# Token products divided around a unit test, with filler products, one-hot rows in one operation, and signs, a table load and casts in other places

## The chip, the cores and the metric

The kernel runs on one core of one Trainium2 chip. The metric is device time of one execution in microseconds. TensorE (PE in the rows; PEld its weight loads), VectorE (DVE), ScalarE (ACT) and GpSimd (POOL) each work through their own queue in program order; SyncE (SP) issues most transfers.

## The reference, cut to what matters

Sparse attention (32-wide blocks, window 16) over 4 x 8 x 768 x 64 gives x of 3072 tokens by 512; a soft mixture of 32 slots in 8 experts follows; then a routed mixture:

```python
xn = x / (norm(x) + 1e-6);  en = emb / (norm(emb) + 1e-6)
logits = xn @ en.T / tau
expert_idx = argmax(logits, axis=1)
gate_w = softmax(logits)[arange(N), expert_idx]
for e in range(E):
    mask = expert_idx == e
    h = maximum(x[mask] @ w1[e], 0.0)
    out[mask] = gate_w[mask, None] * (h @ w2[e])
```

## The kernel before

The first part (to about 186 us) is attention and the soft mixture; the change leaves it alone. It leaves for every token 32 combination weights, transposed and split into parts, in `cT` (128 rows by 3072 tokens), so that x is `cT` times slot outputs, and the hidden layer of the routed part is `cT` times a matrix G with 1024 columns, one per hidden unit. The rest serves one expert for all tokens (an extra loop at the end, L1445 on, runs only for experts beyond the first; here it does not run).

Most units have one sign for all tokens and are folded into a linear part. The unit test finds the others in two levels, by matrix products and one-hot rows. **Level one** (L1126 to L1191): bounds per unit give `flag1`; the rank products `rank1` (L1161, L1163) count flagged units; `places1` (L1168) turns ranks into one-hot rows `OH1`, four 128-wide operations for each of two halves f (L1175), each multiplied by the unit's sign `ngs`; `candidates` (L1181) gathers the flagged columns of G into `Gc`, and `candidates_t` (L1187) the same transposed into `GNc`, with the unit's index and sign beside it. **Level two**: `tile_mm` (L1089) forms the hidden values of 128 candidates for 1024 tokens, six tiles in three double banks; `tile_ev` (L1099) reduces each tile, odd ones as a maximum on VectorE (L1103), even ones as Relu with a sum on ScalarE (L1105). `rank2`, `places2` and `mixed_units` (L1212, L1223, L1232) pick at most 96 mixed units, fetch their rows of w2 by an indirect DMA into `wr` (GpSimd, L1239), and put their columns into `Gm`. `lin` (L1205) is the linear part; its sum over rows, `prs` (L1338), is copied to the last 32 rows of `wr` (L1339).

**Beside the test** runs the routing. `tok` (L1193) has one product per 128 tokens, 24 of 40 columns, for norms and logits; `pl_out` (L1203) copies 12 at a time. `norms(0)`, `norms(1)` (GpSimd) multiply and add up a tree of halvings; `norms(2)` takes the square root (L966), `norms(3)` the reciprocal. `codes(0)` to `codes(6)` make the expert code and the gate: `codes(5)` is an Exp on ScalarE (L985), which needs another function table than the square root, `codes(6)` sums and inverts.

**Output** (L1356): for each of 24 tiles of 128 tokens three products of 512 columns (L1359 to L1361: `hi` by `wmh`, `lo` by `wmh`, `hi` by `wml`), a scaling by the gate, and a store of 256 KB. `mixed(i)` (L1326) makes `hi` and `lo` for 512 tokens. `wmh` and `wml` are `wr` rounded and its rest.

Order: the program has a manual schedule, so each engine runs in the order of the text. Products that serve no result stand in three places: `fill` (L1087), `warm2`, `warm3` (L1349). Filler products read `cT` and write a bank that nobody reads. Banks of PSUM pass from pool to pool tile by tile, so that a product into a reused bank waits for its last reader.

Of the kernel before, what the change touches and what calls it, by code (L numbers as in the profile page):

```python
# [11 lines left out]
F32 = mybir.dt.float32  # L12
# [10 lines left out]
P = 128  # L23
# [18 lines left out]
NPL = 96  # L42
# [94 lines left out]
def tile_kernel(ctx, tc, qT, kTd, vwd, phi, w1, w2, emb, tau, u1, u2, consts, consts2, out):  # L137
# [802 lines left out]
    cbx = fp.tile([P, 1], F32, name="cbx")  # L940
    base = fp.tile([P, 1], F32, name="base")
# [5 lines left out]
    def norms(i):  # L947

        if i < 2:
            for b in range(2 * i, 2 * i + 2):  # L950
                v = lambda a: a.rearrange("p (g j) s -> p g j s", j=2)
                nc.gpsimd.tensor_tensor(
                    out=v(sq[:, 6 * b : 6 * b + 6]),
                    in0=v(pl[:, 6 * b : 6 * b + 6, 0:NSLOT]),
                    in1=ce_all[:, b].rearrange("p (j g) s -> p g j s", g=3),
                    op=ALU.mult,
                )
        if i == 1:
            h = NSLOT // 2
            while h > 1:  # L960
                nc.gpsimd.tensor_add(sq[:, :, 0:h], sq[:, :, 0:h], sq[:, :, h : 2 * h])
                h //= 2
            nc.gpsimd.tensor_add(nrm, sq[:, :, 0], sq[:, :, 1])
        if i == 2:
            nc.vector.tensor_scalar_max(nrm, nrm, 0.0)
            nc.scalar.sqrt(nrm, nrm)  # L966
        if i == 3:
            nc.vector.tensor_scalar_add(nrm, nrm, 1e-6)
            nc.vector.reciprocal(nrm, nrm)
# [95 lines left out]
    junk = hhi[0].rearrange("p a b -> p (a b)")[:, 0:1024]  # L1065
# [6 lines left out]
    with ExitStack() as es:  # L1072
# [25 lines left out]

        def tile_ev(i, ph):  # L1099

            k, j = divmod(i, 3)
            if i % 2:
                nc.vector.tensor_reduce(acc[:, k, j : j + 1], ph, axis=AX.X, op=ALU.max)  # L1103
            else:
                nc.scalar.activation(junk, ph, AF.Relu, accum_out=acc[:, k, j : j + 1])  # L1105
# [20 lines left out]
        def flags(f):  # L1126
# [11 lines left out]
            b2 = lambda a: a.unsqueeze(2).to_broadcast([P, 4, 2])  # L1138
            nc.gpsimd.tensor_tensor(
                out=GN[:, ks, P : P + 2], in0=b2(con2[:, C_U + 4 * f : C_U + 4 * f + 4]), in1=b2(ngs[:, ks]),  # L1140
                op=ALU.mult,
            )

# [24 lines left out]
        def places1(f):  # L1168
            ks = slice(4 * f, 4 * f + 4)
            nc.vector.scalar_tensor_tensor(  # L1170
                out=rk[:, ks], in0=prk1[f][:, 0:4], scalar=1.0, in1=flag1[:, f, 0:4],
                op0=ALU.add, op1=ALU.mult,
            )
            for k in range(4 * f, 4 * f + 4):
                nc.vector.scalar_tensor_tensor(  # L1175
                    out=OH1[:, k], in0=iota, scalar=rk[:, k : k + 1], in1=ngs[:, k : k + 1].to_broadcast([P, P]),
                    op0=ALU.is_equal, op1=ALU.mult,
                )
            fits(cbs[:, f : f + 1], prk1[f][:, 4:5], P, cbs[:, 0:1] if f else cb)
# [7 lines left out]
        def candidates_t(f):  # L1187
            p = pgnc[:, f * (P + 2) : (f + 1) * (P + 2)]
            for k in range(4):
                nc.tensor.matmul(p, OH1[:, 4 * f + k], GN[:, 4 * f + k], start=k == 0, stop=k == 3)  # L1190
            return p  # L1191
# [31 lines left out]
        def places2(t):  # L1223
# [5 lines left out]
                out=OH2[:, t], in0=iota[:, 0:NPL], scalar1=rk2[:, ts], scalar2=None, op0=ALU.is_equal  # L1229
            )  # L1230

        def mixed_units(pf):  # L1232
            pix = pgm[0:NPL, 128:130]
            for t in range(2):
                nc.tensor.matmul(pix, OH2[:, t], GNc[:, t, P : P + 2], start=t == 0, stop=t == 1)
            nc.vector.tensor_scalar(
# [8 lines left out]
            fill(1, pf)  # L1245
# [29 lines left out]
        pls = [pre(4 + h, f"pls{h}")[:, 0 : 12 * NKL].rearrange("p (t x) -> p t x", x=NKL) for h in range(2)]  # L1275
        tok(0, 4)
        rank1(0)
        tok(4, 8)
        rank1(1)
        tok(8, 12)  # L1280
        pl_out(0)
        places1(0)
        tok(12, 18)
        candidates(0)
        places1(1)
        tok(18, 24)
        pl_out(1)
        candidates(1)
        es.close()
        ps2 = es.enter_context(tc.tile_pool(name="ps2", bufs=1, space=PSUM, reuse_waits="tile"))  # L1290
        norms(0)
        codes(0)
        linear_columns()
        norms(1)
        codes(1)
        for i in range(6):
            ph = tile_mm(i)
            tile_ev(i, ph)
            if i in (3, 5):
                if i == 3:  # L1300
                    pgnc = one(0, "pgnc")
                p = candidates_t(i // 4)
                nc.scalar.copy(GNc[:, i // 4], p)
            if i == 4:
                prk2 = dbank(0, "rank2")
                rank2(0)
        prr = one(1, "lin")
        lin(0)
        lin(1)
        rank2(1)  # L1310
        pf = dbank(1, "fill1")[:, 0:512]
        fill(1, pf)
        places2(0)
        places2(1)
        nc.scalar.copy(rs, prr)
        pgm = one(0, "pgm")
        mixed_units(pf)
        norms(2)
        fits(cbx, prk2[:, 2:3], NPL, cbs[:, 1:2])
# [25 lines left out]
    mixed(2)  # L1345
    codes(4)
    pw = bankc(6, "warm3")
    for _ in range(3):
        nc.tensor.matmul(pw, Gm, cTt(0, 512), start=True, stop=True)  # L1349
    nc.scalar.copy(wmh[:, c[0]], wr[:, c[0]])  # L1350
    nc.vector.tensor_copy(wmh[:, c[1]], wr[:, c[1]])
    for i in range(2):
        nc.vector.tensor_tensor(out=wml[:, c[i]], in0=wr[:, c[i]], in1=wmh[:, c[i]].bitcast(F32), op=ALU.subtract)
    codes(6)
    row_weights(cbx)
    for t in range(NTT):  # L1356
# [5 lines left out]
        if t % 4 == 1 and t // 4 + 3 < 6:  # L1362
            mixed(t // 4 + 3)
# [94 lines left out]
```

## Time and profile before

| | us |
|---|---|
| median of three runs | 245.72 (244.62 to 248.24) |
| profiled execution | 246.85 |
| its span, first to last instruction | 245.1 |
| TensorE busy, share of the span | 226.9 (93%) |
| VectorE, ScalarE, GpSimd busy | 150.7, 118.0, 94.2 |
| mean granted TensorE clock | 0.939 of full speed |

The profile is one execution. Its rows show busy times and waits of each engine; the granted clock is the share of TensorE's full speed that the chip gave in a stretch (1.00 or 0.50 here). A wait is put down to the instruction that released it last.

### The profile page before, as it was taken

How to read it: one execution, taken by the hardware profiler on the slowest of the kernel's cores; microseconds unless marked ns; L12 is line 12 of the kernel's file. 1: busy time of each engine (PE TensorE's matmuls, PEld its weight loads, DVE VectorE, ACT ScalarE, POOL GpSimd, SP SyncE). 2: the span in 40 equal slices, each digit the busy share in tenths (PEclk: the TensorE clock that was granted, in tenths of full speed). 3: DMA queues.
4: the chain of work that ended last, by engine and by line, in shares of the span. 5: the costliest groups of instructions: out<-in, count | busy, mean ns of one | idle time of the engine just before them, and what ended most of it. 6: DMA issues, size and time to landing. Idle time of an engine off the chain costs nothing.

```text
span 245.1 us, 7881 instructions
## 1 busy us (share of the span) xinstructions
PE 226.9 (93%) x3025; PEld 151.4 (62%) x3025; DVE 150.7 (61%) x709; ACT 118.0 (48%) x279; POOL 94.2 (38%) x147
## 2 busy tenths in 40 slices
PE   8798999999999999999999999999899999779970
PEld 3476877777768777677777543333254895257850
DVE  2348877769859798688875541128671646376740
ACT  2364466566656657565686311141322735346540
POOL 0264766557574775747663001000013374200000
PEclk9869999999999999999999999999999857758997
DMA  6999999999997999984499999999949400105992
GB/s 199 383 413 367 335 362 334 392 386 361 369 367 260 347 366 397 369 297 150 154 319 342 396 409 394 409 407 408 367 158 379 166 0 0 32 1 214 348 400 79
DMA packets 33658, 72.53 MB, mean 296 GB/s; under 512 B 2712, under 2 KB 4504, under 8 KB 33616
## 3 DMA queue, kind: packets, MB, share of 16 engines
q1 hardware_dynamic: 33552, 71.77, 79.8%
q8 instruction: 26, 0.43, 0.7%
q0 software_dynamic: 64, 0.20, 0.3%
q14 instruction: 16, 0.13, 0.1%
HBM read 65.67 MB, written 6.29 MB: 294 GB/s over the span
## 4 chain that ended last, share of the span: by engine, by line
PE 82%; DMA 7%; DVE 2%; SPq 2%; issue 2%; ACT 2%; POOL 1%; ACTq 0%; POOLq 0%; DVEq 0%
PE po L379 10%; PE s L324 9%; PE pt L366 8%; DMA vw<-in_vw_dram 7%; PE pO L856 6%; PE ph L777 6%; PE tx L412 5%; PE pv L272 4%; PE lp L430 4%; PE py L1359 3%; PE py L1360 2%; PE pd L284 2%; PE py L1361 2%; PE pa L487 2%; PE pls L1195 2%
## 5 line engine op out<-in xcount | busy, mean ns | idle before, releaser
L352 POOL TENSOR_TENSOR fix<-fix,nb 128x360 f32<-128x360 f32 x64 | 49.1, 788 | 49.1 <-DVE nb L339 48.9
L339 DVE CUSTOM_DVE_ANT_0 fix<-s,con 128x120 f32<-128x120 f32 x192 | 41.7, 278 | 18.0 <-PE s L324 14.4
L367 ACT COPY pts<-pt 120x384 f32<-120x384 f32 x64 | 27.7, 482 | 13.5 <-PE pt L366 13.5
L358 ACT ACTIVATE fix<-fix 128x360 f32<-128x360 f32 x64 | 29.1, 508 | 7.0 <-POOL fix L352 6.9
L379 PE MATMUL po<-vw,pts 120*64 120x65 f32 x768 | 30.0, 225 | 1.9 <-POOL vw L290 1.0
L379 PEld LDWEIGHTS po<-vw,pts 120*64 120x64 f32 x768 | 25.4, 137 | 7.6 <-issue 2.7
L366 PE MATMUL pt<-con,fix 128*120 128x128 f32 x192 | 27.9, 282 | 0.9 <-ACT fix L358 0.9
L290 POOL COPY vw<-vw 24x780 f32<-24x780 f32 x31 | 26.7, 861 | 2.0 <-POOL fix L352 0.2
L366 PEld LDWEIGHTS pt<-con,fix 128*120 128x120 f32 x192 | 21.6, 140 | 6.8 <-issue 5.0
L396 DVE TENSOR_TENSOR X<-po,den 128x384 f32<-128x384 f32 x32 | 17.8, 558 | 1.1
L422 ACT COPY xT<-tx 128x384 f32<-128x384 f32 x32 | 15.3, 480 | 6.0 <-PE tx L412 5.2
L324 PE MATMUL s<-fix,fix 64*64 64x120 f32 x480 | 17.8, 278 | 0.0
L412 PE MATMUL tx<-con,X 128*128 128x128 f32 x96 | 16.4, 282 | 0.0
L339 DVE DVE_READ_ACCUMULATOR2_ANT nb<- 128x1 f32 x192 | 16.0, 83 | 0.0
L856 PE MATMUL pO<-w,hx 128*32 128x512 f32 (+1 forms) x152 | 15.4, 510 | 0.0
L300 DVE TENSOR_REDUCE hm<-fix 128x48 f32<-128x768 f32 x16 | 15.1, 944 | 0.4 <-DMA fix<-in_kT_dram 0.4
L777 PE MATMUL ph<-w,siT 128*32 128x512 f32 x128 | 14.8, 596 | 0.4 <-DVE siT L600 0.4
L324 PEld LDWEIGHTS s<-fix,fix 64*64 64x64 f32 x480 | 13.0, 137 | 3.5 <-issue 2.6
L272 PE MATMUL pv<-vw,con 120*32 120x130 f32 x384 | 14.9, 291 | 0.0
L217 POOL TENSOR_TENSOR bm<-bx 32x24 f32<-32x24 f32 x1 | 0.2, 225 | 34.9 <-DVE bx L209 34.9
L412 PEld LDWEIGHTS tx<-con,X 128*128 128x128 f32 x96 | 10.7, 141 | 3.7 <-issue 2.8
L324 PE MATMUL s<-fix 64*64 64x120 f32 x288 | 11.1, 283 | 1.5 <-DMA fix<-in_qT_dram 0.9
(265 smaller groups left out, 357.8 us busy)
## 6 DMA issues: line engine op xcount, KB each, us to landing
w<-in_moe_w_dram SPq DMA_DIRECT2D x30, 1024.0 KB, 9.3
vw<-in_vw_dram SPq DMA_DIRECT2D x32, 390.0 KB, 6.5
fix<-in_kT_dram SPq DMA_DIRECT2D x15, 484.0 KB, 5.1
out_dram<-Y SPq DMA_DIRECT2D x24, 256.0 KB, 2.5
fix<-in_qT_dram SPq DMA_DIRECT2D x15, 384.0 KB, 5.8
w1e<-in_moe_w_dram SPq DMA_DIRECT2D x4, 512.0 KB, 4.4
w2e<-in_moe_w_dram SPq DMA_DIRECT2D x4, 512.0 KB, 8.8
wx<-in_moe_w_dram SPq DMA_DIRECT2D x1, 1024.0 KB, 10.3
```

Source lines behind the costliest of these rows:

```text
L272: nc.tensor.matmul(pv[32 * g : 32 * g + 32, 0:130], con[:KW, b0 : b0 + 32], vw[:KW, par, x0 : x0 + 130], start=c == 0, stop=c == 2,)
L290: (nc.scalar.copy if n == 0 and par else nc.gpsimd.tensor_copy)(st_["vw", n][row0 : row0 + NB, par].rearrange("p (s x) -> p s x", s=6), vo ...
L324: nc.tensor.matmul(sp[j][64 * i : 64 * i + 64, c, :], qns[n % 3][64 * j : 64 * j + 64, 64 * t : 64 * t + 64], kTs[n % 3][64 * j : 64 * j + ...
L339: nc.vector.tensor_tensor_reduce(out=sms[u % 2][:, j, c, :], in0=sp[:, c, :], in1=con[:, m0 : m0 + KW], scale=-0.125, scalar=3.0e38, op0=A ...
L352: nc.gpsimd.tensor_tensor(out=sm, in0=sm, in1=st_["nb", u][:, j].unsqueeze(2).to_broadcast([P, 3, KW]), op=ALU.subtract)
L358: nc.scalar.activation(sm, sm, AF.Exp, scale=-1.0)
L366: nc.tensor.transpose(pt[:, c, :], sms[u % 2][:, j, c, :], ident)
L367: nc.scalar.copy(pts[:, j], pt)
L379: nc.tensor.matmul(po[64 * i : 64 * i + 64, c, j, :], pts[:, j, c, 64 * i : 64 * i + 64], vw[:KW, i, x0 : x0 + 65], start=True, stop=True,)
L412: nc.tensor.transpose(pt[:, c * P : c * P + P], st_["X", b][:, c0 + c, hp * P : hp * P + P], ident)
L777: nc.tensor.matmul(ph[32 * g : 32 * g + 32, :], siT[:, kc, :], w[:, g, :], start=kc == 0, stop=kc == 3)
L856: nc.tensor.matmul(po[c][32 * g : 32 * g + 32, 0 : cs.stop - cs.start], hTs[r][:, fc, 32 * g : 32 * g + 32], w[:, g, cs], start=(r, fc) in ...
```

## The change

The first twelve of the 24 token products stay where they are; the last twelve, which stood around the candidates, go into the tile loop, behind tiles 2 and 3, with the copy and norms of their half. One filler each stands behind `rank1(0)`, `rank1(1)` and ahead of `candidates(0)`. The one-hot rows of level one carry no sign and are one operation per half; the sign stands in a column of its own beside the unit's index (one more small operation on GpSimd per half), and the tests apply it: the Relu by its scale, VectorE by a multiply-and-maximum instead of the maximum. `OH2` gets it too. `candidates_t(0)` goes ahead of the tiles, `candidates_t(1)` behind tile 1. `rank2(1)` stands between the halves of `lin`; two fillers of the last part are gone, and `fits(cbx)` stands ahead of the index. A one-column Exp directly behind the square root brings the table load there. `codes(0)`, `codes(1)` come last in the block. `mixed(2)` to `mixed(5)` all lie in the output loop, three warm products are six, the rounding to `wmh` is one copy on ScalarE, and the rest `wml` is taken after the gate operations.

```diff
@@ -938,6 +938,7 @@
...
     cbx = fp.tile([P, 1], F32, name="cbx")
+    ss1 = fp.tile([P, 1], F32, name="ss1")
     base = fp.tile([P, 1], F32, name="base")
@@ -955,15 +956,16 @@
...
                 )
-        if i == 1:
+            s = sq[:, 12 * i : 12 * i + 12]
             h = NSLOT // 2
             while h > 1:
-                nc.gpsimd.tensor_add(sq[:, :, 0:h], sq[:, :, 0:h], sq[:, :, h : 2 * h])
+                nc.gpsimd.tensor_add(s[:, :, 0:h], s[:, :, 0:h], s[:, :, h : 2 * h])
                 h //= 2
-            nc.gpsimd.tensor_add(nrm, sq[:, :, 0], sq[:, :, 1])
+            nc.gpsimd.tensor_add(nrm[:, 12 * i : 12 * i + 12], s[:, :, 0], s[:, :, 1])
         if i == 2:
...
             nc.scalar.sqrt(nrm, nrm)
+            nc.scalar.activation(ss1, nrm[:, 0:1], AF.Exp)
         if i == 3:
@@ -1062,7 +1064,7 @@
...
     rs = Y[4][:, 0, :]
-    junk = hhi[0].rearrange("p a b -> p (a b)")[:, 0:1024]
+    junk = [hhi[0].rearrange("p a b -> p (a b)")[:, 0:1024], hlo[0].rearrange("p a b -> p (a b)")[:, 0:1024]]
@@ -1096,13 +1098,25 @@
...
+        def sg(k):
+            return GNc[:, k, P + 1 : P + 2].bitcast(F32)
+
         def tile_ev(i, ph):
...
             if i % 2:
-                nc.vector.tensor_reduce(acc[:, k, j : j + 1], ph, axis=AX.X, op=ALU.max)
+                nc.vector.tensor_tensor_reduce(
+                    out=junk[1],
+                    in0=ph,
+                    in1=sg(k).to_broadcast([P, 1024]),
+                    scale=1.0,
+                    scalar=0.0,
+                    op0=ALU.mult,
+                    op1=ALU.max,
+                    accum_out=acc[:, k, j : j + 1],
+                )
             else:
-                nc.scalar.activation(junk, ph, AF.Relu, accum_out=acc[:, k, j : j + 1])
+                nc.scalar.activation(junk[0], ph, AF.Relu, scale=sg(k), accum_out=acc[:, k, j : j + 1])
@@ -1135,11 +1149,10 @@
...
             )
-            b2 = lambda a: a.unsqueeze(2).to_broadcast([P, 4, 2])
             nc.gpsimd.tensor_tensor(
-                out=GN[:, ks, P : P + 2], in0=b2(con2[:, C_U + 4 * f : C_U + 4 * f + 4]), in1=b2(ngs[:, ks]),
-                op=ALU.mult,
-            )
+                out=GN[:, ks, P], in0=con2[:, C_U + 4 * f : C_U + 4 * f + 4], in1=ngs[:, ks], op=ALU.mult
+            )
+            nc.gpsimd.tensor_copy(GN[:, ks, P + 1], ngs[:, ks])
@@ -1171,12 +1184,12 @@
...
             )
-            for k in range(4 * f, 4 * f + 4):
-                nc.vector.scalar_tensor_tensor(
-                    out=OH1[:, k], in0=iota, scalar=rk[:, k : k + 1], in1=ngs[:, k : k + 1].to_broadcast([P, P]),
-                    op0=ALU.is_equal, op1=ALU.mult,
-                )
-            fits(cbs[:, f : f + 1], prk1[f][:, 4:5], P, cbs[:, 0:1] if f else cb)
+            nc.vector.tensor_tensor(
+                out=OH1[:, ks],
+                in0=iota.unsqueeze(1).to_broadcast([P, 4, P]),
+                in1=rk[:, ks].unsqueeze(2).to_broadcast([P, 4, P]),
+                op=ALU.is_equal,
+            )
@@ -1184,11 +1197,10 @@
...
-        def candidates_t(f):
-            p = pgnc[:, f * (P + 2) : (f + 1) * (P + 2)]
+        def candidates_t(f, p):
             for k in range(4):
                 nc.tensor.matmul(p, OH1[:, 4 * f + k], GN[:, 4 * f + k], start=k == 0, stop=k == 3)
-            return p
+            nc.scalar.copy(GNc[:, f], p)
@@ -1226,13 +1238,14 @@
...
             nc.vector.tensor_scalar(
-                out=OH2[:, t], in0=iota[:, 0:NPL], scalar1=rk2[:, ts], scalar2=None, op0=ALU.is_equal
-            )
-
-        def mixed_units(pf):
+                out=OH2[:, t], in0=iota[:, 0:NPL], scalar1=rk2[:, ts], scalar2=sg(t), op0=ALU.is_equal, op1=ALU.mult
+            )
+
+        def mixed_units():
             pix = pgm[0:NPL, 128:130]
...
                 nc.tensor.matmul(pix, OH2[:, t], GNc[:, t, P : P + 2], start=t == 0, stop=t == 1)
+            fits(cbx, prk2[:, 2:3], NPL, cbs[:, 1:2])
             nc.vector.tensor_scalar(
@@ -1242,7 +1255,6 @@
...
             )
-            fill(1, pf)
             for t in range(2):
@@ -1272,51 +1284,55 @@
...
         prk1 = [pre(3 * f, f"prk{f}") for f in range(2)]
-        pls = [pre(4 + h, f"pls{h}")[:, 0 : 12 * NKL].rearrange("p (t x) -> p t x", x=NKL) for h in range(2)]
+        plb = lambda t: t[:, 0 : 12 * NKL].rearrange("p (t x) -> p t x", x=NKL)
+        pls = [plb(pre(4, "pls0"))]
         tok(0, 4)
         rank1(0)
+        fill(1, pf)
         tok(4, 8)
         rank1(1)
+        fill(1, pf)
         tok(8, 12)
...
         places1(0)
-        tok(12, 18)
+        places1(1)
+        for f in range(2):
+            fits(cbs[:, f : f + 1], prk1[f][:, 4:5], P, cbs[:, 0:1] if f else cb)
+        fill(1, pf)
         candidates(0)
-        places1(1)
-        tok(18, 24)
-        pl_out(1)
+        candidates_t(0, pre(6, "pgnc0")[:, 0 : P + 2])
         candidates(1)
+        norms(0)
         es.close()
         ps2 = es.enter_context(tc.tile_pool(name="ps2", bufs=1, space=PSUM, reuse_waits="tile"))
-        norms(0)
-        codes(0)
         linear_columns()
-        norms(1)
-        codes(1)
         for i in range(6):
             ph = tile_mm(i)
+            if i == 1:
+                candidates_t(1, one(0, "pgnc1")[:, 0 : P + 2])
             tile_ev(i, ph)
-            if i in (3, 5):
-                if i == 3:
-                    pgnc = one(0, "pgnc")
-                p = candidates_t(i // 4)
-                nc.scalar.copy(GNc[:, i // 4], p)
+            if i == 2:
+                pls.append(plb(one(1, "pls1")))
+                tok(12, 18)
+            if i == 3:
+                tok(18, 24)
+                pl_out(1)
+                norms(1)
             if i == 4:
...
         lin(0)
+        rank2(1)
         lin(1)
-        rank2(1)
-        pf = dbank(1, "fill1")[:, 0:512]
-        fill(1, pf)
         places2(0)
         places2(1)
+        pgm = one(0, "pgm")
         nc.scalar.copy(rs, prr)
-        pgm = one(0, "pgm")
-        mixed_units(pf)
+        mixed_units()
         norms(2)
-        fits(cbx, prk2[:, 2:3], NPL, cbs[:, 1:2])
+        codes(0)
+        codes(1)
@@ -1342,25 +1358,23 @@
...
     codes(5)
-    mixed(2)
     codes(4)
     pw = bankc(6, "warm3")
-    for _ in range(3):
+    for _ in range(6):
         nc.tensor.matmul(pw, Gm, cTt(0, 512), start=True, stop=True)
-    nc.scalar.copy(wmh[:, c[0]], wr[:, c[0]])
-    nc.vector.tensor_copy(wmh[:, c[1]], wr[:, c[1]])
+    nc.scalar.copy(wmh, wr)
+    codes(6)
+    row_weights(cbx)
     for i in range(2):
         nc.vector.tensor_tensor(out=wml[:, c[i]], in0=wr[:, c[i]], in1=wmh[:, c[i]].bitcast(F32), op=ALU.subtract)
-    codes(6)
-    row_weights(cbx)
     for t in range(NTT):
...
         nc.tensor.matmul(py, hi, wml, start=False, stop=True)
-        if t % 4 == 1 and t // 4 + 3 < 6:
-            mixed(t // 4 + 3)
+        if t % 4 == 1 and t // 4 + 2 < 6:
+            mixed(t // 4 + 2)
         if t % 2:
```

## Rows read from the trace of the kernel before

**Rows 1.** Page, the chain that ended last: shares of the span by engine.

```profile
PE 82%; DMA 7%; DVE 2%; SPq 2%; issue 2%; ACT 2%; POOL 1%; ACTq 0%; POOLq 0%; DVEq 0%
```

**Rows 2.** Stretches: length; busy us of PE, PEld, DVE, ACT, POOL; PEclk; DMA share; GB/s.

```profile
191.10:193.80 2.70, 2.62 (x20) 2.13 (x18) 1.95 (x5) 2.44 (x6) 0.33 (x2) 1.00 0.51 199
...
194.80:200.40 5.60, 5.60 (x32) 5.60 (x32) 2.82 (x11) 1.62 (x4) 3.82 (x10) 0.50 0.00 0
...
200.40:204.90 4.50, 4.50 (x14) 3.54 (x14) 3.16 (x5) 2.49 (x5) 4.11 (x9) 0.50 0.00 0
...
208.60:211.70 3.10, 2.14 (x10) 0.98 (x8) 1.79 (x10) 0.81 (x2) 1.13 (x1) 1.00 0.00 0
...
215.30:218.00 2.70, 1.57 (x5) 0.73 (x3) 1.34 (x5) 1.62 (x4) 0.00 (x0) 0.50 0.01 3
...
218.00:221.90 3.90, 3.90 (x9) 3.06 (x10) 2.22 (x7) 0.58 (x2) 0.00 (x0) 0.50 0.15 60
...
231.00:237.50 6.50, 6.46 (x29) 5.02 (x27) 3.68 (x5) 3.16 (x6) 0.00 (x0) 1.00 1.05 402
```

**Rows 3.** The chain in order of time, from 191 us: start, length, what.

```profile
193.77 0.57 PE pls L1195 x4
...
195.22 2.16 PE pls L1195 x10
...
199.52 0.93 PE pgc L1184 x4
...
200.44 3.53 PE pht L1094 x8
...
206.70 1.85 PE lin L1208 x16
...
217.96 0.76 PE py L1359
...
222.34 0.23 PE py L1359
```

**Rows 4.** Timeline of PE: start, length, line, out<-in, shapes, count, wait.

```profile
208.48 0.18 PE L1217 MATMUL rank<-flag,ltb 128*128 128x1 bf16 x1
...
211.18 1.39 PE L1338 MATMUL prs<-Y,con 128*32 128x512 f32 x2 [0.59 <-DVE cbx L1251]
```

**Rows 5.** Timeline of DVE, 190 to 220 us.

```profile
191.05 0.68 DVE L1120 TENSOR_TENSOR gs<-pgb,gs 32x512 fp32r<-32x512 f32 x1 [4.65 <-ACT gs L1118]
...
206.34 1.22 DVE L1103 TENSOR_REDUCE acc<-pht 128x1 f32<-128x1024 f32 x1 [0.86 <-PE pht L1094]
...
207.86 0.16 DVE L1215 TENSOR_SCALAR flag<-fmx 128x1 bf16<-128x1 f32 x1
...
208.72 0.16 DVE L1225 SCALAR_TENSOR_TENSOR rk<-rank,flag 128x1 f32<-128x1 f32 x1 [0.71 <-PE rank L1218]
...
217.73 0.76 DVE L1353 TENSOR_TENSOR w2l<-scr,w2l 128x256 fp32r<-128x256 f32 x2
...
219.33 0.24 DVE L1016 SCALAR_TENSOR_TENSOR scr<-scr,cbx 128x24 f32<-128x24 f32 x1
```

**Rows 6.** Timeline of ACT, 210 to 217 us.

```profile
211.00 0.22 ACT L966 ACTIVATE scr<-scr 128x24 f32<-128x24 f32 x1 [1.77 <-DVE scr L965]
...
212.60 0.58 ACT L1339 COPY scr<-prs 32x512 f32<-32x512 f32 x1 [1.38 <-PE prs L1338]
...
213.39 1.09 ACT L1331 ACTIVATE hhi<-phm 128x512 fp32r<-128x512 f32 x2 [0.21 <-PE phm L1329]
...
214.49 1.28 ACT L985 ACT_TABLE_LOAD   x1
...
215.78 0.36 ACT L985 ACTIVATE hx<-hx 128x192 f32<-128x192 f32 x1
```

**Rows 7.** Page, groups: line, operation, shapes, count | busy, mean ns | idle before.

```profile
L339 DVE CUSTOM_DVE_ANT_0 fix<-s,con 128x120 f32<-128x120 f32 x192 | 41.7, 278 | 18.0 <-PE s L324 14.4
```

**Rows 8.** Timeline of POOL, 200 to 206 us.

```profile
201.41 2.51 POOL L961 TENSOR_TENSOR Y<-Y 128x384 f32<-128x384 f32 x4
```

## The prediction

> **What bounds the kernel now.** I read the chain that ended last first: 82% of the span is TensorE, so the question is what its queue holds up [rows 1]. Next the stretches from 191 us on, where every changed line lies, with the granted clock beside the busy time [rows 2]. The reader is to see four things. Until 193.8 the clock is at 1.00 (2.4 GHz). From 194.8 to 204.9 us TensorE is busy without a gap and yet at 0.50 (1.2 GHz); it fell among the small token products of L1195. It is back at 1.00 in the stretch from 208.6, but that one is busy for only 2.14 us of 3.10, and the first 3.9 us of the output loop are at 0.50 again. And the loop's end runs at 1.00 with its DMA share at 1.05. Then the chain in order of time gives prices at either level: four token products 0.57 at full, ten 2.16 at low, so 0.14 and 0.216 each; four candidate products 0.93 at low; eight 512-column tile products 3.53 at low, 0.44 each, against 0.23 for one of the output loop at full [rows 3]. Last the timelines: the serial chain from the last tile to the output loop (reduction, rank, one-hot, index, square root, copies), where TensorE [rows 4] takes turns with VectorE [rows 5] and ScalarE [rows 6].
>
> All sums are made against the profiled execution, 246.85 us with a span of 245.1. The median of the runs shown is 245.72, so 1.13 is taken off at the end.
>
> **Front: from the first token product to the last tile product (before: 193.77 [rows 3] to 206.3, where the last tile's reduction begins [rows 5]).** Twelve of 24 token products leave the stretch ahead of the tiles; three fillers and the first transposed candidates (four products) enter it. At low clock: -12 x 0.216 = -2.59, +3 x 0.44 = +1.32, +0.93 (the transposed set priced as the candidates), so -0.3: the tiles begin at 200.44 - 0.3 = 200.1 [rows 3]. The tile loop then holds 12 x 0.44 = 5.3 of tiles, 0.93 of the second transposed set and 2.6 of tokens: 8.8, ending at 208.9, which is 2.6 later than 206.3. Before, the same loop had no tokens, half its transposed products fell behind its end, and the clock rose inside it. At full clock: 24 x 0.14 = 3.4, rank products 0.3 (an estimate from the 0.18 us of one, overlapping [rows 4]), three fillers 0.7, sixteen candidate products priced as tokens 2.2, tiles 12 x 0.23 = 2.8, and some 0.5 in which the rank product inside the loop waits for VectorE: 9.9 from 193.77, or 203.7: 2.6 earlier.
>
> Which of the two? The fillers put a 512-column product behind each four tokens. But the clock fell at the end of a stretch in which 20 products, two of them such fillers and eight of them 112 columns wide, took 2.62 us [rows 2], and what now stands there is three fillers among twelve tokens and ten tiny rank products in about as much time. That is no denser, so I take the low price. The other is a rival.
>
> **From the last tile to the output loop.** Before, the rank product's flag was there at 208.02 [rows 5], but it stood behind all 16 L1208 rows and ran at 208.48 [rows 4]; now half of them stand ahead of it: -0.4. The last reduction becomes a multiply-and-max over 1024 elements. Its price at this size is not in the trace: below, 1.22 as the plain reduction [rows 5]; above, 2.37 if the 278 ns for 120 elements [rows 7] scaled in full. The 32x512 VectorE operation at 0.68 [rows 5] against that 0.278 gives 1.04 ns per element, so 1.22: no change. At low clock the linear products' second half (half of 1.85 [rows 3], doubled) takes 1.85 and would hold the index product 0.85 longer; bounds 0 and 0.85, and I take 0, because the tiles precede it.
>
> Count from the rank's VectorE operation, 208.72 before [rows 5]. Before: square root at +2.28, row copy +3.88, two Relu to +5.76, table load to +7.05, Exp to +7.42 [rows 6], a third Relu and the weight copy, output loop at +9.24 [rows 3]. After: the fit test (0.16, as the rank's operation, which is of its kind) goes ahead of the index: square root at +2.44, done at +2.66. The table load (1.28) and a one-column Exp (priced as the 0.22 of the square root) follow at once: ScalarE is free at +4.16. TensorE's product for the row copy no longer waits for the fit test (before: 0.59, so that it began at 211.18 [rows 4]); it ends by +3.0 at full clock, +3.9 at low, before ScalarE is free. Copy 0.58, two Relu 1.09, Exp 0.36, weight copy 0.58 (now 512 wide, as the row copy) [rows 6]: +6.8. So -2.45. The subtraction of the weights now comes behind the gate operations on VectorE. Those ended 1.08 after the subtraction before (219.57 against 218.49), and it takes 0.76 [rows 5]: ready 1.84 behind the Exp, +8.0, while the first two output products at low clock end at +7.6. The third waits 0.4. Net -2.0. Mixed block 2, taken out of this stretch, puts one product into the loop: +0.2.
>
> Of the table load the row says 1.28, with the Exp starting 0.01 behind it [rows 6]. The Trainium skill (ScalarE: Activation LUTs, What ACT_TABLE_LOAD costs) puts a drain of 1.38 beside the load, 2.66 for a switch; by it the row copy would come 1.38 later and the -2.0 shrink to about -0.6. The row shows no such drain behind the load.
>
> **Covered edits, at nothing.** The one-hot rows become one 512-wide operation, 0.68 as the nearest row [rows 5], in place of four: TensorE is still in tokens and fillers then; if VectorE were awaited there, the tiles would begin up to 0.5 earlier. The norm tree, 2.51 at full width [rows 8], is split: its second half comes behind the second token copy inside the tile loop and has some 3 us until the square root; each microsecond more would move all behind that. One extra sign copy lies on GpSimd too. Codes 0 and 1 move behind the index DMA: only the real Exp waits for them, some 3 us after the square root. The Relu of the test gets a scale operand; that lies beside TensorE's 8.8 even if it cost 0.1 each.
>
> **The output stage.** It runs at low clock from 217.96 [rows 3] to about 221.9: nine products at 0.43 instead of 0.23, a loss of 1.8 [rows 2, 3]. Before, the 2.70 us ahead of it were busy for 1.57, with three warm products [rows 2]; now two mixed and six warm products (8 x 0.44 = 3.5, from +3.9) end at about +7.4, past the loop's start, with no gap. The clock should rise sooner. Bounds 0 and -1.8; I take -1.0.
>
> **Sum.** +2.6 - 0.4 - 2.0 + 0.2 - 1.0 = -0.6: 246.25 for the profiled execution, 245.1 on the scale of the median.
>
> **Rivals.** *The fillers hold the clock.* For it: they are put where the fall began, and the moved half of the tokens fits into a tile loop that at full clock waits for ScalarE and VectorE. Against it: the stretch before the fall. Then -2.6 - 0.4 - 1.7 (the third output product waits 0.75) + 0.2 - 1.8 = -6.3: 239.4, or 241.2 if the output stage keeps its low start. The Trainium skill (TensorE: Matmul & The Clock Gate, Loop structure matters more than you think) holds that matmuls which follow each other at once stay warm and that waits cool them, which would favour this rival; the stretch of 5.60 us busy out of 5.60 at 0.50 does not agree [rows 2].
>
> *Slower: tokens among the tiles keep the clock low through the linear products.* Place: the tile loop, where 12 narrow and 4 candidate products take 3.5 of 8.8. If the clock is not back when the linear products begin (about 209), the price is +2.6 - 0.4 + 0.85 - 2.0 + 0.2 with no gain in the output stage: +1.25, 247.0; and if the warm products then run at full clock and end 2 us before the loop, the fall comes at its start and costs 1.8 more: 248.8.
>
> *The stores take the gain.* At 402 GB/s with a share of 1.05 [rows 2] one 262,144-byte tile needs 0.65 us, TensorE's three products 0.69: room of 0.04 per tile. If stores bound it, the output gain of 1.0 is lost: 246.1. Against it: the loop begins earlier, and so do they.
>
> **Chances.** Forecast 0.45 (243.5 to 246.5), held clock 0.28 (239.4 to 241.5), slower mechanism 0.2 (246.5 to 249), stores 0.07. The range 240.3 to 248.3 leaves out the lower half of the held case and the last of the slower one. Two per cent, about what a measurement of this kernel can tell from no change, is 4.9 us: faster means below 240.8, most of the held case, 0.2; slower means above 250.6, which the slower mechanism reaches only with a multiply-and-max near its upper bound (+1.15) besides, 0.05; within, 0.75.
>
> **What would show it.** Right: granted clock 0.50 over the later half of the first twelve tokens and into the tiles; the last tile product near 208.9; the table load straight behind the square root and beside the row's product; the output loop about 7 us behind the rank operation instead of 9.24. Wrong: a clock of 1.00 from 194 to 204 (the held rival); a multiply-and-max far from 1.22; a ScalarE gap of over a microsecond at the load; the clock low at the linear products (the slower rival).

## The result, and the profile after

The changed kernel takes 246.26 us (median of 20 runs, 240.2 to 249.91), the kernel before 245.78 (20 runs, 244.29 to 249.29). The ratio is 0.9863, with a 95% interval of 0.9827 to 0.9899, so the difference is within 2%. This ratio, like those of the table below, counts only the executions within 1.5% of the fastest of their kernel, here 6 of 21 of the changed kernel and 15 of 20 of the one before (beside e5 to e8 9 of 29). Over all executions the means are 245.78 and 246.33 and the medians differ by 0.48 the other way, so this measurement shows no gain of the change as a whole, but a wider spread. In e1 and e9 below, the same kernel's median is 0.5 and 1.2% lower than before.

The single times fall into two groups by the mean granted clock of the execution: 8 runs of 240.2 to 244.3 us with a clock of 0.973 or more, 13 (with the profiled one) of 245.1 to 249.9 with 0.966 or less. Mean clocks above 0.974 are new: in the 69 executions of the kernel before that ran beside the experiments there are none, of the changed kernel's 39 (these 21, e1 and e9) there are 15. The profile that stands here is of the second group: 249.91 us, span 248.1.

Stretches after (length; busy us of PE, PEld, DVE, ACT, POOL; PEclk; DMA share; GB/s):

```profile
10.00:20.00 10.00, 9.26 (x112) 6.64 (x112) 3.95 (x28) 5.41 (x13) 3.89 (x5) 0.50 1.04 414
...
194.00:197.40 3.40, 3.32 (x29) 2.78 (x28) 2.54 (x10) 3.03 (x9) 1.03 (x5) 1.00 0.45 172
197.40:202.00 4.60, 4.60 (x27) 4.41 (x25) 1.73 (x5) 1.36 (x4) 3.65 (x10) 0.50 0.00 0
...
206.00:211.50 5.50, 5.50 (x25) 4.13 (x27) 1.46 (x5) 2.83 (x5) 1.44 (x3) 0.50 0.00 0
211.50:214.50 3.00, 3.00 (x18) 0.42 (x18) 2.46 (x9) 0.14 (x2) 1.39 (x5) 0.50 0.00 0
214.50:217.00 2.50, 2.12 (x11) 0.74 (x7) 1.14 (x6) 1.12 (x3) 1.11 (x1) 1.00 0.00 0
...
220.70:224.60 3.90, 2.52 (x10) 1.77 (x11) 2.70 (x9) 0.31 (x1) 0.00 (x0) 1.00 0.00 0
...
234.00:240.00 6.00, 6.00 (x28) 4.99 (x27) 3.76 (x6) 3.65 (x6) 0.00 (x0) 1.00 0.98 374
```

The stretch of 10 to 20 us, in code that the change does not touch, of the kernel before, of e11 and of e12 (both described below), in this order:

```profile
10.00:20.00 10.00, 8.85 (x141) 6.58 (x143) 5.31 (x33) 5.10 (x12) 3.89 (x5) 0.66 1.04 413
10.00:20.00 10.00, 8.99 (x134) 6.50 (x133) 4.89 (x33) 5.66 (x13) 3.89 (x5) 1.00 1.03 412
10.00:20.00 10.00, 8.00 (x167) 5.83 (x170) 6.51 (x38) 5.08 (x13) 3.89 (x5) 1.00 1.03 411
```

The chain after, in order of time:

```profile
196.41 0.57 PE pls L1207 x4
197.10 0.35 PE fill L1089
197.45 0.59 PE pls L1207 x4
...
202.55 1.81 PE pht L1096 x4
...
211.46 1.87 PE lin L1220 x8
213.47 1.50 PE lin L1220 x8
...
222.81 0.50 PE py L1375
```

The timeline of VectorE after:

```profile
211.50 1.23 DVE L1108 CUSTOM_DVE_ANT_0 hlo<-pht,gs 128x1024 fp32r<-128x1024 f32 x1 [1.59 <-PE pht L1096]
...
213.51 0.16 DVE L1237 SCALAR_TENSOR_TENSOR rk<-rank,flag 128x1 f32<-128x1 f32 x1 [0.33 <-PE rank L1230]
...
215.34 0.22 DVE L1249 TENSOR_SCALAR idx<-pgm,base 96x1 int32<-96x1 f32 x1 [0.81 <-PE pgm L1247]
...
219.45 1.29 DVE L1348 SCALAR_TENSOR_TENSOR hlo<-phm,hhi 128x512 fp32r<-128x512 f32 x2 [0.71 <-ACT hhi L1347]
220.65 0.34 DVE L985 TENSOR_REDUCE scr<-hx 128x24 f32<-128x192 f32 x1
220.91 0.34 DVE L989 TENSOR_REDUCE scr<-hx 128x24 f32<-128x192 f32 x1
...
222.00 0.76 DVE L1369 TENSOR_TENSOR w2l<-scr,w2l 128x256 fp32r<-128x256 f32 x2
```

The timeline of ScalarE after:

```profile
216.45 0.22 ACT L967 ACTIVATE scr<-scr 128x24 f32<-128x24 f32 x1 [0.79 <-DVE scr L966]
216.69 1.28 ACT L968 ACT_TABLE_LOAD   x1
217.99 0.20 ACT L968 ACTIVATE ss<-scr 128x1 f32<-128x1 f32 x1
218.21 0.58 ACT L1355 COPY scr<-prs 32x512 f32<-32x512 f32 x1
...
219.79 0.36 ACT L987 ACTIVATE hx<-hx 128x192 f32<-128x192 f32 x1
```

The timeline of TensorE after, at the start of the output loop and at its end:

```profile
220.71 0.50 PE L1373 MATMUL py<-w2l,hhi 128*128 128x512 f32 x1 [1.65 <-ACT w2l L1365]
221.05 0.40 PE L1374 MATMUL py<-w2l,hlo 128*128 128x512 f32 x1
222.81 0.50 PE L1375 MATMUL py<-w2l,hhi 128*128 128x512 f32 x1 [1.36 <-DVE w2l L1369]
...
240.09 0.39 PE L1375 MATMUL py<-w2l,hhi 128*128 128x512 f32 x1
```

The first token products and the last output product of the kernel before, in the same view:

```profile
193.72 0.62 PE L1195 MATMUL pls<-KL,cT 128*128 128x40 f32 x4
...
237.07 0.39 PE L1361 MATMUL py<-w2l,hhi 128*128 128x512 f32 x1
```

The clock falls among the tokens and fillers at 197.4 and stays at 0.50 through the tiles (1.81 for four) and almost to the end of the linear products, 17.1 us in all; from 214.5 it is at 1.00, in the output loop too. The reader is to see next that this profile is 3.06 us above the profile before (249.91 against 246.85), and that little of it is the change. The first token product starts at 196.41 against 193.77 [rows 3], 2.64 later, in code that is the same. The clock at 10 to 20 us, 0.50 here and 0.66 before, is not shown to be the cause: e11 and e12 are alike up to the first token, both had the clock at 1.00 until then, and their first tokens came at 197.02 and 193.09. From the first token to the last output product it is 43.73 us (196.36 in the timeline to 240.09) against 43.35 (193.72 to 237.07): +0.38. That +0.38 has four terms:

- first token to the last reduction: 15.09 (196.41 to 211.50) against 12.57 [rows 3, 5], +2.52;
- last reduction to the rank's operation: 2.01 against 2.38 [rows 5], -0.37;
- the rank's operation to the first output product: 7.20 (213.51 to 220.71) against 9.24 [rows 3, 5], -2.04;
- first to last output product: 19.38 against 19.11, +0.27.

### The profile page after: what moved, and what is told of

Same layout as the page of the kernel before. It is cut to its first block, busy times and chain, and to the rows that moved or that the text cites. A ratio compares the mean times of both kernels' runs of the same rounds, so it can differ in the third digit from the quotient of the medians.

```text
span 248.1 us, 7891 instructions
## 1 busy us (share of the span) xinstructions
PE 229.0 (92%) x3029; PEld 152.4 (61%) x3029; DVE 149.6 (60%) x705; ACT 118.6 (48%) x280; POOL 95.8 (39%) x154
## 4 chain that ended last, share of the span: by engine, by line
PE 85%; DVE 4%; ACT 3%; DMA 2%; issue 2%; POOL 2%; SPq 1%; POOLq 0%; DVEq 0%
PE po L379 11%; PE pt L366 9%; PE s L324 9%; PE pO L856 6%; PE ph L777 6%; PE pv L272 5%; PE tx L412 5%; PE lp L430 4%; PE pd L284 3%; PE pht L1096 2%; PE py L1375 2%; PE py L1373 2%; PE pa L487 2%; PE py L1374 2%; DMA con<-in_consts_dram 2%
## 5 line engine op out<-in xcount | busy, mean ns | idle before, releaser
L379 PE MATMUL po<-vw,pts 120*64 120x65 f32 x768 | 30.9, 229 | 2.2 <-POOL vw L290 1.0
L379 PEld LDWEIGHTS po<-vw,pts 120*64 120x64 f32 x768 | 26.1, 140 | 8.3 <-issue 3.3
L366 PE MATMUL pt<-con,fix 128*120 128x128 f32 x192 | 28.5, 285 | 1.1 <-ACT fix L358 0.8
L280 ACT COPY vw<-pv 128x130 f32<-128x130 f32 x16 | 4.3, 268 | 16.6 <-PE pv L272 16.6
```

What stands on the lines that cost most here:

```text
L366: nc.tensor.transpose(pt[:, c, :], sms[u % 2][:, j, c, :], ident)
L379: nc.tensor.matmul(po[64 * i : 64 * i + 64, c, j, :], pts[:, j, c, 64 * i : 64 * i + 64], vw[:KW, i, x0 : x0 + 65], start=True, stop=True,)
```

## The experiments

Twelve runs were made, in three groups of four; each group was measured on its own chip against the kernel before there (medians 245.5, 247.08 and 246.31). My theory: at low clock the changed kernel takes as long as before, at full clock some 4 us less, and the granted clock of the front, not the amount of work, decides. Rivals: the end of the change brings the gain alone; the fillers bring it; the move of the tokens brings it.

This table puts all of them side by side on the stretch that the change touches, from the first token product to the last output product of the profiled execution; so it is free of what varies ahead of the first token, which comes at 192.4 to 197.0 us in these fourteen profiles.

| kernel | stretch, us | clock low at | ratio to before (95%) | median, us |
|---|---|---|---|---|
| before | 43.35 | 194.7 to 204.8, 211.7 to 221.9 | | |
| changed | 43.73 | 197.4 to 214.5 | 0.9863 (0.9827 to 0.9899) | 246.26 |
| e1 changed, again | 43.63 | 193.9 to 211.1 | 0.9891 (0.9838 to 0.9944) | 244.24 |
| e9 changed, again | 39.19 | 213.6 to 217.0 | 0.9854 (0.9798 to 0.9909) | 243.26 |
| e2 5 more fillers | 46.01 | 194.0 to 204.2, 217.9 to 224.7 | 0.9898 (0.983 to 0.9965) | 247.83 |
| e5 7 more fillers | 40.11 | 214.8 to 218.1 | 0.9943 (0.9896 to 0.9989) | 244.09 |
| e6 no fillers | 40.10 | 199.6 to 209.9 | 0.9922 (0.9862 to 0.9982) | 244.85 |
| e10 no fillers, again | 41.13 | 195.4 to 198.7, 212.5 to 219.2 | 0.9899 (0.9825 to 0.9972) | 243.79 |
| e7 tokens back | 44.21 | 197.0 to 203.7, 217.5 to 224.2 | 1.0102 (1.0003 to 1.0201) | 248.34 |
| e3 the end alone | 41.21 | 196.7 to 203.4, 217.2 to 220.5 | 0.9958 (0.9923 to 0.9993) | 244.49 |
| e8 the end, rest first | 38.38 | 196.9 to 203.6 | 0.9949 (0.9888 to 1.001) | 243.46 |
| e4 changed, rest first | 42.57 | 195.9 to 213.0 | 0.9805 (0.9746 to 0.9865) | 246.06 |
| e11 e5, rest first | 37.66 | 211.8 to 215.1 | 0.9887 (0.9825 to 0.9948) | 243.4 |
| e12 e11, 6 more warm | 38.31 | 203.4 to 206.8 | 0.9884 (0.984 to 0.9928) | 242.89 |

The fillers that e5 and its followers have between the two bounds lie ahead of the first token and are not in the stretch.

The rival that the end alone brings the gain is not ruled out. On the chip that ran both, e3 (the front of before with the new end) and e1 (the whole change) come out alike: medians 244.49 and 244.24 against 245.5, means 244.71 and 244.72. And e8, also with the front of before, has the lowest median of its group and five of its twelve mean clocks above 0.974; its stretch of 38.38 is shorter than e9's. What the whole change has beyond e3 and e8 is its lowest times, 240.2 and 240.59 against 243.2 and 241.81.

**The changed kernel twice more.** No edit.

> The changed kernel once more, beside the others. Theory (clock): its front, from the first token product to the first copy of the last tile's reduction, takes 15.1 us in the profile of the change with the clock low from 197.4 to 214.5; where an execution keeps the clock high it takes some 10 us. So single times spread over 240 to 250 us, and the time of an execution falls with its mean granted clock: about 248 at 0.95, 242 at 0.98. Rival (work): the spread has nothing to do with the granted clock, and the front takes about 15 us at any clock.

> The changed kernel again, so that the three below have it on their own chip. Times so far: 240 to 250, in a group of high mean clock (0.973 and more) and one of 0.966 and less. Expected: the same two groups, median 244 to 246. It tells nothing apart by itself; it is the yardstick.

The profile of e1 repeats the one above in another execution: front 15.35 us. Of its six times two, 241.68 and 242.92, have mean clocks of 0.986 and more, four, 244.22 to 248.38, 0.965 or less, roughly as expected. That of e9 is the other case. Its stretches, and its VectorE:

```profile
193.30:196.00 2.70, 2.70 (x29) 2.56 (x29) 2.52 (x10) 1.59 (x5) 2.28 (x8) 1.00 0.03 6
196.00:200.00 4.00, 4.00 (x29) 3.47 (x28) 1.52 (x4) 2.75 (x7) 3.52 (x11) 1.00 0.00 0
200.00:204.80 4.80, 3.40 (x28) 1.73 (x30) 3.00 (x8) 2.22 (x5) 3.88 (x9) 1.00 0.00 0
...
213.60:217.00 3.40, 3.36 (x8) 2.68 (x9) 0.94 (x2) 0.82 (x2) 0.00 (x0) 0.50 0.22 77
```

```profile
202.85 1.23 DVE L1108 CUSTOM_DVE_ANT_0 hlo<-pht,gs 128x1024 fp32r<-128x1024 f32 x1 [0.86 <-PE pht L1096]
...
204.81 0.16 DVE L1237 SCALAR_TENSOR_TENSOR rk<-rank,flag 128x1 f32<-128x1 f32 x1 [0.28 <-PE rank L1230]
...
206.18 0.21 DVE L1249 TENSOR_SCALAR idx<-pgm,base 96x1 int32<-96x1 f32 x1 [0.34 <-PE pgm L1247]
...
211.75 0.34 DVE L989 TENSOR_REDUCE scr<-hx 128x24 f32<-128x192 f32 x1
...
212.84 0.75 DVE L1369 TENSOR_TENSOR w2l<-scr,w2l 128x256 fp32r<-128x256 f32 x2
```

The same instructions, from 193.28 to 202.85, take 9.57 us here and 15.09 above. Of e9's twelve times seven lie at 240.6 to 243.9 with a mean clock of 0.978 or more, five at 245.2 to 246.9 with 0.973 or less. One kernel does both, from one execution to the next.

**The fillers, more and fewer.** e2 makes the three fills two each and adds one behind each product group of the first candidates; e5 also makes the fill between the two bounds four instead of two; e6 and e10 take the three new fillers out.

```diff
 e2    rank1(0); fill(1 -> 2, pf)      rank1(1); fill(1 -> 2, pf)
       fill(1 -> 2, pf); candidates(0); +fill(1, pf); candidates_t(0, ..); +fill(1, pf)
 e5    as e2, and  bounds(0); fill(2 -> 4, pf)
 e6    -fill(1, pf)   three times
```

> The change with two fillers instead of one at each of the three places and one more behind candidates(0) and behind candidates_t(0): five more products of 512 columns, 1.2 us at full clock, 2.2 at low. Clock theory: the clock stays at 1.00 over the token products, the front falls from 15.1 to about 11 us, and the median falls from 246 to about 242.5, with a smaller spread. Rival (the fillers cannot hold it, they are only work): clock 0.50 as before and 2.2 us more, about 248.5.

> The fillers of the run with five more, and four instead of two between the two sets of bound products: seven more products of 512 columns than the change, 1.6 us at full clock. In the profile of the run with five more the clock was low from 194.0, so it had fallen on the strength of what stands ahead of the token products. Clock theory: with that stretch denser too, few executions or none lose the clock; the two groups of times (about 241 to 244 and 246 to 250) become one, near 243, with mean clocks of 0.98. Rival (fillers do not decide the fall): two groups again, the upper one at 249 to 251.

> The change without its three fillers. Clock theory: every execution loses the clock over the token products, so no time below 243.5 and mean clocks of 0.96 or less; the low group itself gets shorter by 3 x 0.44 = 1.3 us, so 245 to 248, median 246.3. Rival (fillers do not decide): the same share of executions at a mean clock of 0.975 and more, all of them 0.7 to 1.3 us shorter than the change: median about 244.5.

> The change without its three fillers, on the chip of the change. Theory now (one filler per four tokens is too little to decide the fall, and costs 0.7 to 1.3 us): the same share of high mean clocks as the change, and a median 0.5 to 1.3 lower. Rival (the three fillers do save some executions): fewer mean clocks above 0.973 than the change and a median at least as high.

e2 by itself was a miss: its clock fell at 194.0, its six times run from 242.47 to 250.25, and their median of 247.83 is near the rival's 248.5. Two of them also show that the mean clock alone does not give the time: 247.01 at 0.980 and 250.25 at 0.973. e5 kept the clock through the front:

```profile
193.80:196.80 3.00, 3.00 (x30) 2.75 (x30) 2.61 (x10) 1.47 (x4) 2.49 (x10) 1.00 0.02 5
196.80:201.00 4.20, 4.20 (x30) 3.63 (x29) 1.36 (x2) 2.26 (x7) 3.59 (x9) 1.00 0.00 0
```

Nine of its twelve times lie at 243.4 to 244.7. So the spread is narrower than the changed kernel's in its three measurements (it did not run on this chip), at a price: seven more products of 0.23 are 1.6 us at full clock. Without any of the three fillers (e6, e10) the times still reach 241.85 and 241.86, and on the chip that ran both, e10's interval overlaps e9's. e6 had been expected to have no time below 243.5, and two of its twelve lie below. e10's median, expected 0.5 to 1.3 below the changed kernel's, is 0.53 above e9's, and three of its six mean clocks are above 0.973, seven of e9's twelve. The three fillers make no difference that these runs can tell; what separates e2 from e5 in single executions isn't settled, with six times of e2.

**The last twelve tokens back ahead of the tiles**, all else as changed.

```diff
-        pls = [plb(pre(4, "pls0"))]
+        pls = [plb(pre(4, "pls0")), plb(pre(7, "pls1"))]
...
+        tok(12, 18)
         fill(1, pf)
         candidates(0)
+        tok(18, 24)
         candidates_t(0, pre(6, "pgnc0")[:, 0 : P + 2])
+        pl_out(1)
         candidates(1)
...
+        norms(1)
         for i in range(6):
...
-            if i == 2:
-                pls.append(plb(one(1, "pls1")))
-                tok(12, 18)
-            if i == 3:
-                tok(18, 24)
-                pl_out(1)
-                norms(1)
```

> The change with the last twelve token products back around the candidates, ahead of the tiles, all else as in the change, fillers too. Theory (tokens among the tiles delay the clock's return): at low clock the tile loop is then tiles and four products only, 6.2 instead of 8.8 us, and the clock returns inside it; front about 13.5 instead of 15.1 us, upper group near 246. At full clock the tokens no longer lie beside the copies of the tiles and cost up to 1.4: lower group near 243. Rival (where the tokens stand does not matter): the two groups of the change, 240 to 244 and 246 to 250.

Slower than before by 0.03 to 2.0%; no time below 245.55, no mean clock above 0.968, so the expected lower group near 243 did not appear. The front, 194.12 to 207.43, is 13.3 us, near the 13.5 expected, but the clock falls again 1.3 us behind the first output product (216.12):

```profile
200.00:203.30 3.30, 3.30 (x14) 2.87 (x13) 0.34 (x2) 1.67 (x3) 3.06 (x7) 0.50 0.00 0
...
217.30:221.00 3.70, 2.78 (x7) 2.21 (x8) 1.62 (x4) 0.24 (x1) 0.00 (x0) 0.51 0.10 33
221.00:224.10 3.10, 3.10 (x9) 2.43 (x8) 1.40 (x2) 1.62 (x3) 0.00 (x0) 0.50 0.51 192
```

So with the fillers and the transposed candidates ahead of the tiles, the tokens seem better placed among the tiles. With six times, an interval that begins at 0.03%, and no run of the changed kernel on this chip, that is likely and not shown.

**The end alone, and the rest of the weights first.** e3 has the front of before and the end of the change (fit test ahead of the index, table load behind the square root, warm products, copies, order of the weights). e4 is the changed kernel with the subtraction of the weights ahead of the gate operations, e8 is e3 with the same edit.

```diff
-    codes(6)
-    row_weights(cbx)
     for i in range(2):
         nc.vector.tensor_tensor(out=wml[:, c[i]], ...)
+    codes(6)
+    row_weights(cbx)
```

> The kernel before with the end of the change alone: table load behind the square root, fit test ahead of the index, rank between the linear halves, no fillers there, mixed block 2 in the output loop, six warm products, one cast, rest behind the gate. Theory: 2.0 us less from the rank operation to the output loop, minus what the third output product waits for the rest (1.4 to 1.8 in the profile of the change), minus 0.2 for the product in the loop, plus up to 1.8 if the clock rises sooner: 245.7 - 0.5 to - 2.0, so 243.7 to 245.2. Rival (the end gains nothing, all of the difference is in the front): 245.7.

> The change with the subtraction of the rest of the weights ahead of the gate operations on VectorE, as the kernel before had it. Theory: the third output product no longer waits 1.36 us for the rest (it waited until 222.81 with the first at 220.71), so the output loop runs on 1.0 to 1.4 us sooner, and the median falls by about 1.0 against the change. Rival: the gate is then late and the first scaling waits for it, or the stores bound the loop, and the time stays within 0.3.

> The kernel before with the end of the change, and the rest of the weights ahead of the gate operations. Theory: the end alone gave 244.5 against 245.5 with the third output product waiting; without that wait another 1.0 to 1.3: 243.3, in a narrow spread, since its front has the clock low in every execution. Rival: the wait was hidden behind the stores or a low clock: 244.5.

The end alone is worth 0.4% (0.07 to 0.77). Its median of 244.49 lies in the 243.7 to 245.2 expected, and e8's 243.46 is near its 243.3, though not in a narrow spread (241.81 to 245.86). With the edit the third output product waits 0.27 in place of 1.36. TensorE of e4:

```profile
219.42 0.50 PE L1373 MATMUL py<-w2l,hhi 128*128 128x512 f32 x1 [1.63 <-ACT w2l L1365]
219.76 0.40 PE L1374 MATMUL py<-w2l,hlo 128*128 128x512 f32 x1
220.42 0.50 PE L1375 MATMUL py<-w2l,hhi 128*128 128x512 f32 x1 [0.27 <-DVE w2l L1367]
```

From the first output product to the third it is 1.00 us here and 2.10 above, and the stretch of e4 is 1.1 to 1.2 shorter than the two of the changed kernel with the same 17.1 us at low clock (42.57 against 43.63 and 43.73). The median, expected 1.0 lower, does not show it: 246.06 in seven times against e1's 244.24. In e3 and e8, which differ in this edit alone, the front has the same 6.8 us at low clock, but in e3 the clock falls again 3 us behind the first output product:

```profile
217.30:220.70 3.40, 3.40 (x10) 2.66 (x9) 1.75 (x3) 1.18 (x2) 0.00 (x0) 0.52 0.31 120
```

and in e8 it does not:

```profile
216.00:220.00 4.00, 4.00 (x18) 3.30 (x19) 3.52 (x8) 1.87 (x3) 0.00 (x0) 1.00 0.31 115
```

First to last output product: 20.94 us in e3 (214.26 to 235.20), 18.25 in e8 (214.98 to 233.23); 1.1 of the 2.7 is the wait, the rest the clock. In the four profiles where 0.27 is left of the wait (e4, e8, e11, e12) the loop runs at full clock; of the nine with all of it, six (e2, e3, e5, e7, e9, e10) lose the clock 0.8 to 3.0 us behind the first output product and three (changed, e1, e6) don't; one profile of each is too few to call the wait the cause. The ratios do not separate e3 from e8, which ran on different chips, and e4's times split as the changed kernel's do (239.58 to 241.41, 246.06 to 247.73).

**All of it together.** e11 is e5 with the rest first; e12 has twelve warm products ahead of the loop in place of six.

> The run with seven more fillers, and the rest of the weights ahead of the gate operations. In that run the third output product waited from 213.84 to 215.19, the clock fell at 214.9 and the output loop began at 0.50. Theory: without the wait the loop runs on 1.36 sooner, and in some executions the clock does not fall there: 242.0 to 243, against 244.1. Rival: the fall at the start of the output loop has other causes (2 us without a product ahead of the loop) and takes the 1.36 back: 243.5 to 244.

> The same with twelve warm products instead of six ahead of the output loop: at full clock they end at about 212.7 in the time scale of the run with seven more fillers, where the loop began at 213.1, so they cost nothing there and leave no stretch without products. Theory: the clock stays at 1.00 into the output loop in nearly every execution, one narrow group near 241. Rival: where the clock is low anyway, twelve products take 5.3 us and push the loop back by 2: no better than the run before, 242 to 244, with single times above 246.

e11's front holds the clock; the low stretch comes at 211.8 to 215.1, ahead of the loop. e12's comes at 203.4 to 206.8, under the linear products:

```profile
203.70:206.40 2.70, 2.70 (x15) 0.53 (x18) 1.86 (x6) 0.00 (x0) 1.69 (x5) 0.50 0.00 0
```

On this chip the medians are 246.31 before, 243.26 changed, 243.4 and 242.89: no version beats the changed kernel by more than the intervals leave open. e11's median lies between its theory (242.0 to 243) and its rival (243.5 to 244); e12's lies in its rival's 242 to 244, and the one narrow group near 241 did not come. The spread looks narrower, which six and twelve times do not settle: e11 ends at 244.8, e12 at 245.85 with seven of twelve times in 241.7 to 243.0, the changed kernel there at 246.86.

## Why the prediction was right, point by point

**The front, +2.6 forecast, +2.52 measured** in the low case, and the held rival's 9.9 us was 9.57 in e9. Both prices were right; what was wrong is that they stood as two answers of which one would be true. They are two cases of one kernel. The Trainium skill (TensorE: Matmul & The Clock Gate, Loop structure matters more than you think), by which matmuls behind one another stay warm, agrees with e9 (4.00 busy of 4.00 at 1.00) and not with the profile after (4.60 of 4.60 at 0.50).

**The last tile to the rank, -0.4 forecast, -0.37.** The multiply-and-max over 1024 took 1.23 with 0.08 behind it for its result, against 1.22 taken (the two rows as printed give 1.03 ns per element, not 1.04, and 1.21); the bound of 2.37 was far off. **The table load** runs 0.02 behind the square root, takes 1.28, and the one-column Exp follows 0.02 later (216.69 + 1.28 to 217.99). The drain that the Trainium skill (ScalarE: Activation LUTs, What ACT_TABLE_LOAD costs) adds does not show here; with it the time to the row copy would have been 1.38 longer.

**The rank to the output loop, +6.8 forecast: 6.73 at full clock** (204.81 to 211.54 in e9), **7.20 at low.** The difference is the bound 0 to 0.85 that I set at 0: with the linear products at low clock (1.87 and 1.50 for eight each) the index came 1.83 behind the rank's operation, 1.37 in e9. I took 0 because the tiles precede the linear products, and that reason was wrong in this case: the tiles, busy without a gap, did not bring the clock back. A low clock at the linear products was the sign set for the slower rival, and 0.46 of its price did come. Its other half did not: the clock rose at 214.5 and stayed up.

**The third output product, the term that was mis-sized.** Forecast: the rest of the weights ready 1.84 behind the Exp, a wait of 0.4 at low clock and 0.75 at full. Measured: 1.36 of idle in each. The 1.84 itself was right; it was counted from the wrong point. The Exp ended at 220.15, but the gate's reduction (L989) started at 220.91, because VectorE still had the two 512-wide low parts (L1348, 1.29 from 219.45) and the reduction of L985 in its queue. That is 0.76 in the profile after and 0.77 in e9 (210.98 to 211.75). The step that failed is the one that listed what the wait stood behind: it named the gate operations and not the work ahead of them. e4 and e8, with the subtraction ahead of the gates, have 0.27 left of the wait.

**The output stage, -1.0 forecast.** In the profile after, no product of the loop is at low clock, -1.8; but the wait takes 1.6 of it (2.10 from the first product to the third, where two products at full clock are 0.46) and the extra mixed product 0.23. These add up to +0.07; first to last is +0.27, and the other 0.2 is not placed. In e9 the loop does lose the clock (3.4 us, from 2.0 us behind its first product), much as the prediction's case of a held front with a low start has it: that sum gave -4.5, and e9's stretch is 4.16 shorter than before (39.19 against 43.35).

**The sum.** 245.1 forecast as the median; measured 246.26, and 244.24 and 243.26 in e1 and e9, all in the range of 240.3 to 248.3. On the stretch of the profile after, the forecast of -0.6 came out as +0.38: 0.4 of the miss is the index behind the linear products, 0.7 the wait and the loop. That the median still lies in the forecast case's 243.5 to 246.5 is in part luck: the single times of the first measurement lie in every case (two in the held rival's 239.4 to 241.5, five in the forecast's, seven in the slower rival's 246.5 to 249), and three medians of one kernel differ by 3.0. The stores were no limit: the share at the loop's end was 0.98 at 374 GB/s, with TensorE busy for 6.00 of 6.00 us.

What is open: why one execution keeps the clock in the front and the next does not. The stretch of 10 to 20 us does not decide it: its clock was 1.00 in e1 and in e9, of which e1 lost the clock in the front and e9 did not. Seven more fillers (e5, e11, e12) kept it in the front of all three profiles (in e12 until 0.6 us before its end), but what in them does it was not taken apart. Open too is what moves the first token by up to 4.6 us in code that hardly differs, nearly as much as the 5.5 us between the two fronts (15.09 and 9.57).

## What to carry to other kernels

Price TensorE's work at both clock levels, and expect one kernel to do both: look at the spread and the clock of the single times before a median is explained, and compare the touched stretch, not the span. Where a wait is moved behind other work, count it from when its engine is free of everything queued ahead, not from the releasing instruction. Work that only the third consumer needs, but which it needs at once, goes ahead of work that is needed later (here the subtraction of 0.76 ahead of the gates: 1.1 us of the stretch, though no median shows it).

## What the runs showed of the hardware

TensorE can be busy without a gap and yet stay at the low clock: 17.1 us at 0.50 in the profile after, with 4.60 busy of 4.60 and 5.50 of 5.50. It can also keep the clock with gaps: 3.40 busy of 4.80 at 1.00 in e9. The wide linear products, 3.00 of 3.00 us busy with almost no weight loads (0.42), were still at 0.50, and the clock rose only about their end. And in each of the four profiles that held the clock in the front it fell later: in e9 and e5 soon behind the start of the output loop, in e12 under the linear products, in e11 ahead of the loop, for 3.3 to 3.4 us each in the table.
